# Reading the moving operand of split matmuls as four interleaved sets of 16-byte lines, with the weights at another address

## The chip, the cores and the metric

The kernel runs on one core of one Trainium2 chip. The metric is the device time of one execution in microseconds. Before the change it is 2151.36 us, the median of 3 runs (2151.3 to 2151.45).

## What is computed

Four batches of a channel attention are followed by a feed-forward layer. All data are float32.

```
B, N, C = 4, 6080, 256;  d_ff = 2048
qn = q / (norm of q over the rows + 1e-6);  kn likewise      # per batch and channel
s  = kn^T @ qn / tau                                         # 256 x 256 per batch
a  = softmax of s over its last axis
x  = v @ a                                                   # 6080 x 256 per batch
h  = x @ w_in                                                # 256 -> 2048
out = (h - tanh(h)) @ w_out                                  # 2048 -> 256
```

## The kernel before, in words

The kernel never forms x. For each batch it folds the attention matrix into the first weight (a @ w_in), so that the main loop multiplies v by a folded weight, applies h - tanh(h), and multiplies by w_out.

The work is cut into 192 slots: 4 batches, 6 pairs of column blocks of v, 8 slices of d_ff. A pair holds two blocks of 512 columns; the sixth pair of a batch holds two of 480. In one slot the first product is done as seven products of 128 x 128 weights with sums of v blocks (Strassen's scheme with Winograd's sums; `p1` to `p7` in `Quad.product`), which leave four results in the PSUM banks called x, y and z. ScalarE and VectorE add them up, apply tanh and the subtraction, and split the result g into two parts. The second product (`second`, L1173) multiplies the four results by w_out in 24 matmuls and gathers in the four banks ps_o.

Precision is kept by a split format: a float32 number is the sum of a high and a low part, both of type float32r (hi and lo tiles; gh and gl for g, f for the folded weight, wo_h and wo_l for w_out). A product of two split operands is three matmuls: high by low, high by high, low by high (`products`, L341 to L350). One slot thus issues 7 x 3 + 24 = 45 matmuls in the split format, each behind a weight load (LDWEIGHTS) of its own. A matmul streams its moving operand (128 partitions x 512 columns of 4 bytes) past the 128 x 128 weights that were loaded and writes 512 columns of one PSUM bank. Both the moving operand and the bank are walked in plain order of their columns before the change.

Other split matmuls are beside the slots: the scores s of later batches (ps_s, 256 columns wide, weights and moving operand both out of the tiles qh and ql), and the folding of later batches in groups (ps_w in `group_product`, 512 wide, weights in ef). Scores of batch 0 and some of batch 1 use plain float32 operands instead (the branch `wl is None` in `products`).

All weights and moving operands of the main loop lie, before the change, at multiples of 256 bytes in their partition; the unused tile `pad` (PAD = 208 floats) behind two small tiles sees to that. The folded weights come back from DRAM for each slot (`load_fold`, L835) into a ring of three buffers f.

The order of all instructions on all engines is written out by a planner (class `Plan`) at build time: it gives each instruction a price (`pe_cost` for matmuls, `act_cost`, `dve_cost`), a due time, and walks through the queue of each engine. The prices decide only the order. The order of the slots' products is fixed by the table ORDER; scores and other fills are put where the planner sees TensorE short of work.

Of the kernel before, what the change touches and what calls it, by code (L numbers as in the profile page):

```python
# [10 lines left out]
F32 = mybir.dt.float32  # L11
F32R = mybir.dt.float32r
# [6 lines left out]
P = 128  # L19
SQ = 32  # L20
GJ = 2
NMAX = 512
# [7 lines left out]
NS = 7  # L30
# [18 lines left out]
LEAD = 12  # L49
KEPT = 50.0  # L50
FIRST = 3
PAD = 208
LAG = 30
NORMS = 18

# [223 lines left out]


def pe_cost(n):
    return 0.0134 + n * 0.000417


@with_exitstack
def attn_moe(ctx: ExitStack, tc: tile.TileContext, qk, v4, qkT, tau, w_in, w_out, outT):
# [7 lines left out]
    B, N, _, C = qk.shape  # L294
    KC = C // P
    DFF = 2 * P * w_in.shape[0]
    NS2 = DFF // (2 * P)
# [5 lines left out]
    while s0 < N:  # L303
        n = min(NMAX, (N - s0) // 2)
# [7 lines left out]
    const = ctx.enter_context(tc.tile_pool(name="const", bufs=1))  # L312
# [4 lines left out]
    f_p = ctx.enter_context(tc.tile_pool(name="f_p", bufs=1))  # L317
    e_p = ctx.enter_context(tc.tile_pool(name="e_p", bufs=1))
# [3 lines left out]
    ring = {  # L322
        "wi": Ring(3), "f": Ring(3), "fa": Ring(1), "fb": Ring(1), "raw": Ring(3), "qh": Ring(2), "ql": Ring(2), "nt": Ring(2),
        "vraw": Ring(1), "vt": Ring(1), "vhl": Ring(8),
        "u": Ring(3), "c": Ring(4), "t": Ring(4), "gh": Ring(5), "gl": Ring(5), "ob": Ring(2),
    }

    def sb(pool, tag, shape, dtype, name):
        return pool.tile(list(shape), dtype, tag=tag, name=name, bufs=ring[tag].bufs)

    def bank(i, name, shape=(P, 512)):

        return ps_p.tile(list(shape), F32, tag=f"bank{i}", name=name)
# [3 lines left out]
    ones = const.tile([P, P], F32, name="ones")  # L337
    nc.vector.memset(ones, 1.0)

    def products(out, terms, first, last):  # L340

        seq = []
        for (wh, wl), (xh, xl) in terms:
            seq += [(wh, xh)] if wl is None else [(wh, xl), (wh, xh), (wl, xh)]
        for i, (w, x) in enumerate(seq):
            ins = nc.tensor.matmul(  # L346
                out, w, x,
                start=first and i == 0, stop=last and i == len(seq) - 1,
                skip_group_check=True,
            )  # L350
        return ins
# [3 lines left out]
    itau = const.tile([P, 1], F32, name="itau")  # L355
    const.tile([P, PAD], F32, name="pad")

# [7 lines left out]
        nc.vector.reciprocal(itau, ps_tau[0][:, 0:1])  # L365


    wo_h = const.tile([P, 2 * NS2, C], F32R, name="wo_h")
    wo_l = const.tile([P, 2 * NS2, C], F32R, name="wo_l")
    WN = 512  # L370

    class Convert:
# [74 lines left out]
    while j < NJ:  # L447
        n = min(GJ, NJ - j) if j >= SINGLES else 1
# [10 lines left out]
    class Attn:  # L459
# [218 lines left out]
                    nc.tensor.transpose(self.pt[:, kk, m * P:(m + 1) * P], self.e[:, m, kk * P:(kk + 1) * P], ident)  # L678

        def take_hi(self):  # L680
            self.ef = e_p.tile([P, 2, NS, P], F32R, name="ef")
            self.eh, self.el = (
                self.ef[:, j].rearrange("p n f -> p (n f)")[:, 0:KC * C].rearrange("p (k c) -> p k c", k=KC) for j in range(2)
            )
            nc.scalar.copy(self.eh, self.pt)
# [5 lines left out]
            nc.vector.tensor_scalar(self.e[:, m, :], self.e[:, m, :], self.rs[:, m:m + 1], None, op0=ALU.mult)  # L691

        def forms_hi(self):
            self.ef = e_p.tile([P, 2, NS, P], F32R, name="ef")
            nc.scalar.copy(self.ef[:, 0], self.fxe[:, 0:NS, :])

        def forms_lo(self):
# [69 lines left out]
        def fold_hi(self, s, part):  # L767
            gs = self.b * SLOTS + s
            if gs not in fold:
                fold[gs] = sb(f_p, "f", [P, 2, NS, P], F32R, f"f_{gs}")  # L770
            nc.scalar.copy(fold[gs][:, 0, part], self.fx[s][:, part, :])

        def fold_lo(self, s, part):
# [8 lines left out]
    fold = {}  # L782

    def where(gs):
        return gs // SLOTS, gs % SLOTS // NS2, gs % NS2
# [45 lines left out]

    def load_fold(gs):
        b, p, s = where(gs)
        fold[gs] = sb(f_p, "f", [P, 2, NS, P], F32R, f"f_{gs}")
        nc.sync.dma_start(fold[gs].bitcast(F32), fold_d[b, s])  # L835


# [45 lines left out]
    def plan_fold(b, s, z):  # L883
# [4 lines left out]
        for low, e in enumerate((a.ebuf, a.lbuf)):  # L888
            plan.add("PE", (8 - 4 * low) * pe_cost(FB), lambda low=low: a.fold(s, z, low), reads=[w, e], writes=[pw])
# [60 lines left out]
    def plan_group_product(b, group, k, z):  # L950
        a = ats[b]
        w = formbuf.pop((b, group, k))
        pw = Buf(z)
        which, _, takes = GROUP[k]
        name = f"{group}_{k}"
        plan.add("PE", 3 * pe_cost(NMAX), lambda: a.group_product(which, forms.pop((b, group, k)), z, name), reads=[w, a.ebuf, a.lbuf], writes=[pw])
        for to, plus in takes:
            fresh = (k, to) in ((0, (0, 0)), (1, (0, 1)))
            if fresh:
                a.fxbuf[to[1]] = Buf(ring[("fa", "fb")[to[1]]])  # L960
            plan.add(
                "DVE" if plus else "ACT", (dve_cost if plus else act_cost)(NMAX),
                lambda to=to, plus=plus, fresh=fresh: a.group_take(name, to, plus, fresh),
                reads=[pw] + ([a.fxbuf[plus[1]]] if plus and plus[1] != to[1] else []), writes=[a.fxbuf[to[1]]], port=False,
            )
# [176 lines left out]
    outs = {}  # L1142
    obufs = {}

    def second(quad, i):

        b, p, s, n = quad.b, quad.p, quad.s, quad.n
        row, c = i // 10 - 1, i % 10 - 1
        f = 2 * s + row
        gh, gl = quad.bufs["g", i]  # L1150
        key = b, p, c
        first = key not in obufs
        if first:
            obufs[key] = [0] + [Buf(3 + 2 * c + m) for m in range(KC)]
        done = obufs[key]
        done[0] += 1
        last = done[0] == 2 * NS2

        parts = (0, 1, 0, 0), (0, 0, 0, 1), (1, 1, 0, 0), (1, 0, 0, 1), (1, 0, 1, 2), (0, 0, 1, 2)
        end = last and b == B - 1 and p == NP - 1  # L1160
        if end:
            parts = parts[0:2] + parts[5:6] + parts[2:5]
        whole = slice(0, n)
        pieces = {m: [(whole, done[1 + m])] for m in range(KC)}
        if end and c:
            pieces[1] = [(slice(i * n // 2, (i + 1) * n // 2), Buf(f"end{i}")) for i in range(2)]
        todo = [(m, part, x, j, at_, to) for m, part, x, j in parts[0:3] for at_, to in pieces[m]] if end else []
        todo += [(m, part, x, j, at_, to) for at_, to in pieces[1] for m, part, x, j in parts[3:]] if end else [(m, part, x, j, whole, done[1 + m]) for m, part, x, j in parts]
        for m, part, x, j, at_, to in todo:
            def run(m=m, part=part, x=x, j=j, at_=at_):  # L1170
                if first and j == 0:
                    outs[key + (m,)] = bank(3 + 2 * c + m, f"ps_o_{b}_{p}_{c}_{m}")
                nc.tensor.matmul(  # L1173
                    outs[key + (m,)][:, at_], (wo_l if part else wo_h)[:, f, m * P:(m + 1) * P], quad.g[i][x][:, at_],
                    start=first and j == 0, stop=last and j == 2, skip_group_check=True,
                )

            plan.add("PE", pe_cost(at_.stop - at_.start), run, reads=[gl if x else gh, wobuf[s]], writes=[to])
            yield
        if last:  # L1180
            to_ = b * N + pairs[p][0] + c * n
            for m in range(KC):
                for k, (at_, src) in enumerate(pieces[m]):
                    ob = Buf(ring["raw" if c else "ob"])
                    tiles = {}

                    def copy(copy, m=m, k=k, at_=at_, tiles=tiles):
                        w = at_.stop - at_.start
                        if c:
                            raw = sb(qk_p, "raw", [P, GJ, 2, C], F32, f"ob_{b}_{p}_{c}_{m}_{k}")  # L1190
                            tiles[0] = raw[:, 0].rearrange("p x c -> p (x c)")[:, 0:w]
                        else:
                            tiles[0] = sb(g_p, "ob", [P, NMAX], F32, f"ob_{b}_{p}_{c}_{m}_{k}")[:, 0:w]
                        copy(tiles[0], outs[key + (m,)][:, at_])  # L1194

                    e = "ACT" if (m and len(pieces[m]) == k + 1) or not b and p < 2 else "DVE"
                    plan.add(
                        e, (act_cost if e == "ACT" else dve_cost)(at_.stop - at_.start),
                        lambda e=e, copy=copy: copy(nc.scalar.copy if e == "ACT" else nc.vector.tensor_copy),
                        reads=[src], writes=[ob],  # L1200
                    )
                    plan.add(
                        "SP", 0.35, lambda m=m, at_=at_, tiles=tiles: nc.sync.dma_start(outT[m * P:(m + 1) * P, to_ + at_.start:to_ + at_.stop], tiles[0]),
                        reads=[ob], size=0.26, due=plan.pe_time + 8.0,
                    )
# [248 lines left out]
    for gs in range(TOTAL):  # L1454
        quad = quads.pop(gs)
        for what in beside.get((gs, "start"), ()):
            what()
        for name, then in ORDER:
# [6 lines left out]
            for x in then:  # L1465
                if isinstance(x, int):
                    lag, x = max(0, lag - x), max(0, x - lag)
# [48 lines left out]
```

## Time and profile before

| what | value |
|---|---|
| median of 3 runs | 2151.36 us |
| span of the profiled execution, first to last instruction | 2150.2 us |
| time around the span (median less span) | 1.2 us |
| TensorE busy with matmuls | 2144.7 us, 100% of the span |
| VectorE busy | 1797.3 us, 84% |
| ScalarE busy | 1522.7 us, 71% |
| granted TensorE clock | 1.000 (2.4 GHz) |

[...] What one matmul costs is the distance between two starts. The chain of waits gives it at once: a piece of so many matmuls of one kind, divided by their number.

### The profile page before, as it was taken

What the parts mean: (1) busy time and instruction counts of PE and PEld (TensorE: products, weight loads), DVE (VectorE), ACT (ScalarE), POOL (GpSimd) and SP (SyncE); (2) the same over time, 40 slices, a digit from 0 to 9 for tenths busy, and PEclk for the clock granted to TensorE, in tenths of its full rate; (3) what the DMA queues carried; (4) which work ended last, traced back from release to release, by engine and by line L of the source; (5) the groups of instructions that cost most, each with busy time, mean ns of one, the idle gap of its engine ahead of it and who ended that gap; (6) DMA issues with size and microseconds to landing.
All of it is one profiled execution on the core that took longest, in us unless ns stands there. A gap on an engine that the chain in (4) does not pass through costs nothing.

```text
span 2150.2 us, 28567 instructions
## 1 busy us (share of the span) xinstructions
PE 2144.7 (100%) x9859; PEld 1803.2 (84%) x9859; DVE 1797.3 (84%) x2959; ACT 1522.7 (71%) x2729; POOL 3.3 (0%) x11
## 2 busy tenths in 40 slices
PE   9999999999999999999999999999999999999999
PEld 8888888888888888888888888888888888888888
DVE  7998888899888787788988778878889878778776
ACT  5667788767677777766767778766676666666665
POOL 0000000000000000000000000000000000000000
PEclk9999999999999999999999999999999999999999
DMA  9855576455564555425656445443464432332331
GB/s 386 301 194 185 170 284 241 145 192 194 186 251 173 188 179 188 176 98 182 220 174 247 165 184 208 155 165 112 169 240 160 157 125 89 139 125 86 134 113 53
DMA packets 99907, 383.55 MB, mean 178 GB/s; under 512 B 11442, under 2 KB 20146, under 8 KB 97202
## 3 DMA queue, kind: packets, MB, share of 16 engines
q1 hardware_dynamic: 99762, 381.73, 49.5%
q8 instruction: 78, 1.28, 0.2%
q14 instruction: 67, 0.55, 0.1%
HBM read 315.88 MB, written 65.80 MB: 178 GB/s over the span
## 4 chain that ended last, share of the span: by engine, by line
PE 99%; DMA 0%; SPq 0%; DVE 0%; ACT 0%; issue 0%
PE ps_o L1173 48%; PE x L346 24%; PE y L346 12%; PE ps_s L346 7%; PE z L346 6%; PE ps_w L346 1%; PE ps_w L744 1%; DMA vhl<-qk_dram 0%; SPq L526 0%; PE ps_n L518 0%; PE ps_b L628 0%; PE ps_t L678 0%; DVE ob L1194 0%; ACT ob L1194 0%; PE ps_tau L362 0%
## 5 line engine op out<-in xcount | busy, mean ns | idle before, releaser
L346 PE MATMUL x<-v,f 128*128 128x512 f32 (+1 forms) x2304 | 613.7, 388 | 0.0
L1173 PE MATMUL ps_o<-gh,wo_h 128*128 128x512 f32 (+1 forms) x1537 | 595.6, 388 | 0.0
L1173 PE MATMUL ps_o<-gh,wo_l 128*128 128x512 f32 (+1 forms) x1537 | 595.2, 387 | 0.0
L1107 DVE TENSOR_TENSOR gl<-t,gh 128x512 fp32r<-128x512 f32 (+1 forms) x768 | 516.5, 680 | 90.6 <-ACT gh L1103 87.6
L1103 ACT CAST gh<-t 128x512 fp32r<-128x512 f32 (+1 forms) x768 | 468.9, 618 | 145.4 <-DVE t L1099 136.7
L346 PEld LDWEIGHTS x<-v,f 128*128 128x128 f32 x2304 | 432.3, 188 | 87.2 <-ACT fa L753 0.4
L1095 ACT ACTIVATE t<-c 128x512 f32<-128x512 f32 (+1 forms) x576 | 361.7, 628 | 190.1 <-DVE c L1083 184.9
L1173 PE MATMUL ps_o<-gl,wo_h 128*128 128x512 f32 (+1 forms) x1537 | 471.5, 388 | 0.0
L1099 DVE TENSOR_TENSOR t<-c,t 128x512 f32<-128x512 f32 (+1 forms) x576 | 392.1, 682 | 92.0 <-ACT t L1095 82.8
L1173 PEld LDWEIGHTS ps_o<-gh,wo_l 128*128 128x128 f32 x1537 | 288.6, 188 | 56.9
L1173 PEld LDWEIGHTS ps_o<-gl,wo_h 128*128 128x128 f32 x1537 | 288.6, 188 | 56.5
L1173 PEld LDWEIGHTS ps_o<-gh,wo_h 128*128 128x128 f32 x1537 | 288.7, 188 | 55.6
L346 PE MATMUL y<-v,f 128*128 128x512 f32 (+1 forms) x1152 | 321.6, 387 | 0.0
L1067 ACT COPY u<-x 128x512 f32<-128x512 f32 (+1 forms) x384 | 223.5, 582 | 130.1 <-PE x L346 128.5
L1083 DVE TENSOR_TENSOR c<-u,y 128x512 f32<-128x512 f32 (+1 forms) x384 | 259.5, 676 | 20.6 <-ACT u L1067 10.8
L346 PEld LDWEIGHTS y<-v,f 128*128 128x128 f32 x1152 | 216.2, 188 | 43.1
L1095 ACT ACTIVATE t<-x 128x512 f32<-128x512 f32 (+1 forms) x192 | 113.9, 593 | 97.8 <-PE x L346 97.3
L1099 DVE TENSOR_TENSOR t<-x,t 128x512 f32<-128x512 f32 (+1 forms) x192 | 131.3, 684 | 60.1 <-ACT t L1095 58.8
L1083 DVE TENSOR_TENSOR c<-p,z 128x512 f32<-128x512 f32 (+1 forms) x192 | 130.5, 680 | 51.7 <-PE z L346 47.8
L346 PE MATMUL z<-v,f 128*128 128x512 f32 (+1 forms) x576 | 160.9, 387 | 0.0
L346 PEld LDWEIGHTS z<-v,f 128*128 128x128 f32 x576 | 108.1, 188 | 21.6
L1067 ACT COPY p<-x 128x512 f32<-128x512 f32 (+1 forms) x192 | 112.0, 584 | 2.3 <-PE x L346 0.9
(139 smaller groups left out, 1444.6 us busy)
## 6 DMA issues: line engine op xcount, KB each, us to landing
f<-f_d SPq DMA_DIRECT2D x184, 896.0 KB, 4.6
nt<-qkT_dram SPq DMA_DIRECT2D x96, 380.0 KB, 5.4
raw<-qk_dram SPq DMA_DIRECT2D x47, 512.0 KB, 5.8
wf<-wf_d SPq DMA_DIRECT2D x42, 512.0 KB, 4.0
f_d<-fe SPq DMA_DIRECT2D x48, 448.0 KB, 3.5
vraw<-v_dram SPq DMA_DIRECT2D x20, 1024.0 KB, 7.6
outT_dram<-ob SPq DMA_DIRECT2D x80, 256.0 KB, 3.0
vhl<-qk_dram SPq DMA_DIRECT2D x14, 512.0 KB, 9.2
```

The source lines that it names most:

```text
L346: ins = nc.tensor.matmul(out, w, x, start=first and i == 0, stop=last and i == len(seq) - 1, skip_group_check=True,)
L744: nc.tensor.matmul(self.pw[s][:, m, :], e[:, kk, m * P:(m + 1) * P], w[:, x, kk, :], start=not (low or m or kk or x), stop=bool(low and m ...
L1067: nc.scalar.copy(self.tiles[to], self.tiles["X"][:, 0:self.n])
L1083: nc.vector.tensor_add(self.tiles[i], self.tiles[u], self.tiles[ps][:, 0:self.n])
L1095: nc.scalar.activation(self.tiles["t", i], self.tiles[c][:, 0:n], AF.Tanh)
L1099: nc.vector.tensor_sub(x, self.tiles[c][:, 0:n], x)
L1103: nc.scalar.copy(self.g[i][0], self.tiles["t", i])
L1107: nc.vector.tensor_sub(self.g[i][1], self.tiles["t", i], self.g[i][0].bitcast(F32))
L1173: nc.tensor.matmul(outs[key + (m,)][:, at_], (wo_l if part else wo_h)[:, f, m * P:(m + 1) * P], quad.g[i][x][:, at_], start=first and j == ...
```

## The change

A helper `in_sets` turns 512 columns into four sets. Set 0 holds columns 0 to 3, 16 to 19, 32 to 35 and so on, set 1 columns 4 to 7, 20 to 23 and so on: four columns of 4 bytes are a line of 16 bytes, and a set takes every fourth line. A split matmul then streams set 0, 1, 2 and 3 one after another, and writes the columns of the bank in that same order, so that each result lies where it lay before. The number of matmuls, their widths and their operands are the same. Only split matmuls are changed; those with plain float32 operands, and the folding of batch 0 at L744, keep the plain order.

The tiles of the weights (f, ef, wo) are made a little longer and their contents begin 4 floats in; with PAD, `pad_wo` and `pad_f` all weights of the slots and of the group products then lie 48 bytes past a multiple of 256, while the moving operands stay at multiples of 256. The weights of the scores (qh, ql) stay at multiples of 256 too. wo_h and wo_l become two halves of one tile.

The planner's price of a 512-wide matmul falls by 0.0067 us, which changes the order that it writes.

```
-PAD = 208
+PAD = 24
+SHIFT = 4
...
 def pe_cost(n):
-    return 0.0134 + n * 0.000417
+    return (0.0067 if n == NMAX else 0.0134) + n * 0.000417
...
+    def in_sets(x):
+        return x.rearrange("p (a b c) -> p b a c", b=4, c=4)
...
             ins = nc.tensor.matmul(
-                out, w, x,
+                *((out, w, x) if wl is None else (in_sets(out), w, in_sets(x))),
...
-    wo_h = const.tile([P, 2 * NS2, C], F32R, name="wo_h")
-    wo_l = const.tile([P, 2 * NS2, C], F32R, name="wo_l")
+    def shifted(pool, extra, shape, **named):
+        pitch = 1
+        for x in shape:
+            pitch *= x
+        t = pool.tile([P, pitch + extra], F32R, **named)
+        return t[:, SHIFT:SHIFT + pitch].rearrange("p (a n f) -> p a n f", a=shape[0], n=shape[1])
+
+    wo = shifted(const, 16, (2, 2 * NS2, C), name="wo")
+    wo_h, wo_l = wo[:, 0], wo[:, 1]
+    const.tile([P, 40], F32, name="pad_wo")
+    f_p.tile([P, 8], F32, name="pad_f")
...
-            self.ef = e_p.tile([P, 2, NS, P], F32R, name="ef")
+            self.ef = shifted(e_p, 8, (2, NS, P), name="ef")
...
-        fold[gs] = sb(f_p, "f", [P, 2, NS, P], F32R, f"f_{gs}")
+        fold[gs] = shifted(f_p, 64, (2, NS, P), tag="f", name=f"f_{gs}", bufs=ring["f"].bufs)
...
                 nc.tensor.matmul(
-                    outs[key + (m,)][:, at_], (wo_l if part else wo_h)[:, f, m * P:(m + 1) * P], quad.g[i][x][:, at_],
+                    in_sets(outs[key + (m,)][:, at_]), (wo_l if part else wo_h)[:, f, m * P:(m + 1) * P], in_sets(quad.g[i][x][:, at_]),
```

On TensorE the order of the matmuls changes in one place, in slots 1 and 2 of batch 0. In the rows, x, y, z and ps_o are banks, v, gh and gl moving operands, ps_s the scores of batch 1 (a step is four records of plain float32). Before:

```order
L346 MATMUL x_0_0_1_703<-v5_0_0_563,f_1_635 128x512 x3
L346 MATMUL ps_s_1_393<-qh_1_15_642 128x256 x4
L346 MATMUL x_0_0_2_836<-v0_0_0_478,f_2_675 128x512 x3
L1173 MATMUL ps_o_0_0_1_1_811<-gh22_0_0_0_727,wo_h_95 128x512
L346 MATMUL y_0_0_1_753<-v6_0_0_487,f_1_635 128x512 x3
```

and now:

```order
L350 MATMUL x_0_0_1_704<-v5_0_0_564,f_1_636 128x4x32x4 x3
L350 MATMUL x_0_0_2_820<-v0_0_0_479,f_2_676 128x4x32x4 x3
L1186 MATMUL ps_o_0_0_1_1_810<-gh22_0_0_0_728,wo_95 128x4x32x4
L350 MATMUL y_0_0_1_754<-v6_0_0_488,f_1_636 128x4x32x4 x3
L1186 MATMUL ps_o_0_0_1_1_810<-gl22_0_0_0_741,wo_95 128x4x32x4
```

The score step with qh_1_15 moved from before the first product of slot 2 to before that of slot 3. On ScalarE, VectorE and the DMA queue the same instructions stand in an order that differs by a place or two here and there. VectorE in slot 1, before (c is a sum of banks, t the tanh and then g, gl the low part of g, a_wo the conversion of w_out):

```order
L1099 TENSOR_TENSOR t11_0_0_1_768<-c11_0_0_1_758,t11_0_0_1_768 128x512
L1083 TENSOR_TENSOR c22_0_0_1_796<-u3_0_0_1_775,y_0_0_1_753 128x512
L394 TENSOR_SCALAR a_wo1_788<-a_wo1_788 128x512
L395 SCALAR_TENSOR_TENSOR a_wo1_788<-raw_wo1_470,a_wo1_788 128x512
L1107 TENSOR_TENSOR gl11_0_0_1_813<-t11_0_0_1_768,gh11_0_0_1_799 128x512
```

and now:

```order
L1096 TENSOR_TENSOR c22_0_0_1_788<-u3_0_0_1_770,y_0_0_1_754 128x512
L1112 TENSOR_TENSOR t11_0_0_1_785<-c11_0_0_1_762,t11_0_0_1_785 128x512
L407 TENSOR_SCALAR a_wo1_790<-a_wo1_790 128x512
L408 SCALAR_TENSOR_TENSOR a_wo1_790<-raw_wo1_471,a_wo1_790 128x512
L1120 TENSOR_TENSOR gl11_0_0_1_816<-t11_0_0_1_785,gh11_0_0_1_807 128x512
```

The sum c22 moved ahead of the subtraction t11.

## Rows read from the trace of the kernel before

**Rows 1.** The page's head: span, busy time of TensorE (PE) and VectorE (DVE)

```profile
span 2150.2 us, 28567 instructions
PE 2144.7 (100%) x9859; PEld 1803.2 (84%) x9859; DVE 1797.3 (84%) x2959; ACT 1522.7 (71%) x2729; POOL 3.3 (0%) x11
```

**Rows 2.** Waits of PE: who for whom, total us, times, longest

```profile
PE warm L1383 <- DVE ones L338: 1.1, 1, 1.1
PE ps_s L346 <- DMA vhl<-qk_dram: 0.5, 1, 0.5
```

**Rows 3.** The page's chain that ended last, share of the span by engine

```profile
PE 99%; DMA 0%; SPq 0%; DVE 0%; ACT 0%; issue 0%
```

**Rows 4.** The chain in order of time: start us, length us, what, matmuls

```profile
72.51 3.45 PE ps_s L346 x16
...
157.52 2.04 PE ps_o L1173 x9
...
749.30 1.43 PE ps_s L346 x12
750.74 0.93 PE ps_o L1173 x4
...
2134.59 1.95 PE ps_o L1173 x9
```

**Rows 5.** PE's groups by shape: line, operands, shapes, count, busy us, mean ns

```profile
L346 PE MATMUL x<-v,f 128*128 128x512 f32 x1920 | 515.4, 390 | 0.0
L1173 PE MATMUL ps_o<-gh,wo_h 128*128 128x512 f32 x1280 | 498.6, 390 | 0.0
...
L346 PE MATMUL y<-v,f 128*128 128x512 f32 x960 | 269.6, 389 | 0.0
L346 PE MATMUL z<-v,f 128*128 128x512 f32 x480 | 134.8, 389 | 0.0
L346 PE MATMUL x<-v,f 128*128 128x480 f32 x384 | 99.4, 378 | 0.0
L1173 PE MATMUL ps_o<-gh,wo_h 128*128 128x480 f32 x255 | 96.5, 378 | 0.0
...
L346 PE MATMUL ps_s<-qh,ql 128*128 128x256 f32 x198 | 56.0, 283 | 0.0
...
L346 PE MATMUL y<-v,f 128*128 128x480 f32 x192 | 51.9, 378 | 0.0
L346 PE MATMUL ps_w<-wf,ef 128*128 128x512 f32 x126 | 35.6, 391 | 0.0
...
L346 PE MATMUL z<-v,f 128*128 128x480 f32 x96 | 26.0, 379 | 0.0
```

**Rows 6.** Weight loads (PEld) by shape: count, busy us, mean ns

```profile
L346 PEld LDWEIGHTS x<-v,f 128*128 128x128 f32 x2304 | 432.3, 188 | 87.2 <-ACT fa L753 0.4
...
L346 PEld LDWEIGHTS ps_s<-vhl 128*128 128x128 f32 x120 | 23.1, 195 | 4.8 <-DMA vhl<-qk_dram 1.6
```

**Rows 7.** Busy time by stretch: us, then each engine's busy us (instructions), clock, DMA

```profile
50.00:200.00 150.00, 150.00 (x729) 128.08 (x728) 145.69 (x277) 105.24 (x195) 0.52 (x1) 1.00 0.65 234
120.00:130.00 10.00, 10.00 (x47) 8.57 (x46) 9.86 (x21) 5.57 (x10) 0.00 (x0) 1.00 0.39 127
350.00:400.00 50.00, 50.00 (x223) 41.39 (x222) 48.30 (x86) 39.67 (x77) 0.00 (x0) 1.00 0.69 249
```

**Rows 8.** The page's DMA issues: count, KB each, median us to landing

```profile
f<-f_d SPq DMA_DIRECT2D x184, 896.0 KB, 4.6
```

More of the change, by code (lines that the diff above doesn't have):

```diff
@@ L693, in forms_hi @@
         def forms_hi(self):
-            self.ef = e_p.tile([P, 2, NS, P], F32R, name="ef")
+            self.ef = shifted(e_p, 8, (2, NS, P), name="ef")
             nc.scalar.copy(self.ef[:, 0], self.fxe[:, 0:NS, :])
@@ L833, in load_fold @@
         b, p, s = where(gs)
-        fold[gs] = sb(f_p, "f", [P, 2, NS, P], F32R, f"f_{gs}")
+        fold[gs] = shifted(f_p, 64, (2, NS, P), tag="f", name=f"f_{gs}", bufs=ring["f"].bufs)
         nc.sync.dma_start(fold[gs].bitcast(F32), fold_d[b, s])
```

## The prediction

> **What bounds the kernel now.** I read the page's head first: PE is busy for 2144.7 us of a span of 2150.2 us [rows 1]. Such a share can hide waits, because a matmul's record lasts longer than its turn; so the waits of PE come next. There are two, 1.6 us in all, both in the first microseconds [rows 2], and the chain that ended last is 99% PE [rows 3]. PE is never short of work. The time is the sum of the distances between starts of matmuls, and a change to that distance is worth its full size until another engine takes over. VectorE with 1797.3 us is the nearest, 347 us below PE over the whole run [rows 1], though not in every stretch [rows 7].
>
> Next I ask what one matmul costs and how much of it is columns. The granted clock is 1.00, the 2.4 GHz level [rows 7], so a column takes 0.4167 ns. The chain in order of time gives the distances [rows 4]:
> - 512 wide, split: 2.04 us for 9 is 226.7 ns. The columns take 213.3, so 13.3 ns are excess, 32 cycles.
> - 480 wide, split: 1.95 us for 9 is 216.7 ns. Columns 200.0, excess 16.7.
> - 256 wide, split: 1.43 us for 12 is 119.2 ns. Columns 106.7, excess 12.5.
> - 256 wide, plain float32: 3.45 us for 16 is 215.6 ns. That is two cycles per column, 213.3, and an excess of 2.3.
>
> Two things stand out. The excess of the split matmuls does not grow with the width, so it belongs to the matmul or to its weight load, not to the columns. And it is not one fixed price: right behind the 256-wide run four 512-wide matmuls take 0.93 us, 232.5 ns each [rows 4], and the 480-wide ones pay more than the 512-wide. The plain matmuls, which take an element in only every second cycle, pay almost nothing for the same 512 bytes of weights. This looks like a collision: the next weights are read while the moving operand streams at one element per cycle, and what the two readers lose depends on where each of them is. 128 weights of 4 bytes are 32 lines of 16 bytes, and 32 cycles are lost. I infer it; no row shows a memory.
>
> [...]
>
> **The change part by part.** *Streaming in four sets, weights 48 bytes off.* It touches these matmuls [rows 5]: 512 wide, 1920 of x, 960 of y, 480 of z, 126 of ps_w and three groups of 1280 of ps_o (one is shown): 7326. 480 wide: 384 of x, 192 of y, 96 of z and three groups of 255 of ps_o: 1437. 256 wide: three groups of 198 of ps_s, 594.
>
> What can be won lies between nothing and the excess. All of it down to the plain matmuls' 2.3 ns would be 11.0 ns x 7326 = 80.6 us, 14.4 x 1437 = 20.7 us and 10.2 x 594 = 6.1 us: 107 us. The other end is below nothing, since no row shows a matmul that streams or writes anything but plain columns; its price is under the third rival. If the excess is collisions, a set helps like this: while one set streams (128 columns, 53 ns), only every fourth line of the weights can be in its way. A load is recorded with 188 ns [rows 6], 3.5 sets long, so it meets several sets, but each of them with a quarter of its lines. If each line met its own set once only, 8 of the 32 cycles would stay, a gain of 10 ns. But the 480-wide and the post-score rows show that phases wander and cost up to 19 ns. No row decides between nothing and 10 to 13 ns. I take the middle of the excess, 6.7 ns: 7326 x 6.67 = 48.9 us. The 480-wide sets are 120 columns long and their phases wander already; I give them half of that, 3.3 x 1437 = 4.8 us, with bounds of 0 and 20.7. The scores' weights stay where they were; I give them nothing (0 to 6.1).
>
> *Weight loads.* 188 ns per load [rows 6] stays under the new 220 ns distance, so loads don't take over. The start at 48 bytes leaves 32 lines of 16 bytes. I cost it at nothing.
>
> *Writing the folded weights off the 256 mark.* The DMA of f now lands at 48 bytes past. It takes 4.6 us [rows 8]; a slot is 45 x 226.7 ns = 10.2 us, and f is asked for two slots ahead in a ring of three. Even twice as long it would be covered.
>
> *The planner's order.* PE's list differs in one score step that goes a slot later; the step depends on nothing that is late, and PE is not idle there: nothing. VectorE's, ScalarE's and the DMA queue's lists differ by neighbours that changed places, such as the sum c22 ahead of t11. What hides these is the slack of VectorE and ScalarE, so I look where there is none: in 50 to 200 us VectorE is busy for 145.7 of 150 us, and in 120 to 130 us for 9.86 of 10 [rows 7]. That stretch has 729 matmul records, so PE would gain at most 729 x 6.67 ns = 4.9 us there, and VectorE has 4.3 us to give, but not in each slot. I let 3 us of the gain be lost there as waits of PE for VectorE, and 1 us in stretches like 350 to 400 us, where VectorE is at 48.3 of 50 and PE's 50 fall to 50 - 223 x 6.67 ns = 48.5. Elsewhere (VectorE at 84% on the mean) 2 or 3% less PE time leaves room.
>
> *Sum.* Against the span of the profiled execution: 2150.2 - 48.9 - 4.8 + 4 = 2100.5 us. The median of the runs is 1.2 us above the span, so the forecast is 2101.7, say **2102 us**. Its own range, from 5 to 8.5 ns per 512-wide matmul with 480-wide between 0 and 8 ns, is 2082 to 2119.
>
> **Rivals.**
> *1. Nearly all of the excess goes.* For it: plain matmuls show that the weights can be loaded for 2.3 ns. Against: they take an element every second cycle, which leaves gaps that a split matmul hasn't. Price: 107 us less; in the 150 us stretch PE would need up to 729 x 11.0 ns = 8 us less, 142, below VectorE's 145.7, so I put the waits at 8 us there and elsewhere. 2151.4 - 107 + 8 = 2052 us. Chance 0.12.
>
> *2. The excess is a fixed price of changing weights.* Then sets change nothing, and the time stays at 2151, at most 2 us above from an order that was planned for a faster PE. For it: 32 cycles recur at 512 and, nearly, at 256 columns. Against: the 232.5 and the 216.7 ns rows, and the plain matmuls, which change weights as often. Chance 0.10.
>
> *3. Jumping costs more than colliding: slower.* Before, a matmul reads and writes one run of 2048 bytes; now it makes 128 jumps on both sides, one behind every fourth column. If each costs one cycle, 0.417 ns, a 512-wide matmul pays 53.3 ns, a 480-wide 50.0, a 256-wide 26.7: 391 + 72 + 16 = 479 us, 2630 us. It decides from a small size on: with the forecast's 6.7 ns won, the kernel is slower as soon as a matmul loses 7.3 ns to its jumps, 18 cycles over 128 jumps. The far end is a matmul at two cycles per column, as the plain ones run [rows 4]: 7326 x 213 ns is 1.56 ms more. For it: no row has a broken pattern on PE, so nothing excludes it. Against: within a jump's length the 16 bytes are still read in one piece, and PE at one element per cycle crosses from line to line just as often as before. Chance 0.18.
>
> [...]
>
> **How the numbers follow.** Forecast 0.60, nearly all 0.12, fixed price 0.10, jumps 0.18. A measurement of this kernel tells from no change what is over 0.2%, 4.3 us. Faster is the forecast and the first rival, 0.72; same is the second, 0.10; slower the third, 0.18. The range holds 8 in 10 with the forecast, the fixed price and most of the first rival: 2055 to 2153 us. What it leaves out is nearly all the third.
>
> **What would show it.** Right: pieces of nine ps_o at 1.98 us in place of 2.04, nine 480-wide ones at about 1.92, the 256-wide at 119 ns as before, still no waits of PE beyond a few us, and those between 50 and 200 us on VectorE. Wrong: nine ps_o at 2.04 (fixed price), at 1.94 (nearly all gone), or above 2.04 (jumps); or the shorter distance with PE's share well below 99% and waits for VectorE all over, by which the sum's 4 us would be the step that failed.

## The result and the profile after

The changed kernel takes 2114.66 us, the median of 4 runs (2113.9 to 2116.3), against 2151.38 before: a ratio of 0.983, with a 95% interval of 0.9816 to 0.9844. It is 36.7 us faster. The forecast was 2102 us, 49.7 us faster. The time lies inside the stated range and in the upper part of the forecast's own, which reached to 2119.

The head and the chain's shares of the changed kernel's page (they answer to [rows 1] and [rows 3]):

```profile
span 2112.1 us, 28460 instructions
PE 2103.7 (100%) x9859; PEld 1804.1 (85%) x9859; DVE 1795.8 (85%) x2959; ACT 1523.8 (72%) x2729; POOL 3.3 (0%) x11
...
PE 93%; DVE 5%; ACT 1%; DMA 1%; issue 0%; SPq 0%; ACTq 0%
```

The span fell by 38.1 us and PE's busy time by 41.0; VectorE (DVE) works as long as before. PE is still what the time is made of, but 7% of the chain now runs through other engines. The chain in order of time gives the distances, as in [rows 4] (start us, length us, what, matmuls):

```profile
92.77 1.87 PE ps_o L1186 x8
...
749.34 1.40 PE ps_s L350 x12
750.73 0.91 PE ps_o L1186 x4
...
755.61 1.98 PE ps_o L1186 x9
...
2096.40 1.98 PE ps_o L1186 x9
```

Nine 512-wide matmuls take 1.98 us in place of 2.04: 220.0 ns each, 6.7 ns less. Nine 480-wide ones (the last row) also take 1.98, where they took 1.95: 220.0 ns, 3.3 ns more. The twelve of the scores fell from 1.43 to 1.40. The four behind them need 0.91 us, 228 ns each: the 512-wide distance is not yet back at 220. And the first row shows a stretch that holds another distance: behind twelve matmuls of the folding of batch 0, 45 512-wide matmuls in a row, from 88.9 to 99.4 us, stand 233.3 ns apart.

The waits of PE, all of them (us in total, times, longest us), and the busy stretch (they answer to [rows 2] and [rows 7]):

```profile
PE ps_w L350 <- ACT fx L744: 1.1, 3, 0.4
PE warm L1396 <- DVE ones L339: 1.1, 1, 1.1
PE x L350 <- PE x L350: 0.9, 3, 0.3
PE ps_s L350 <- DMA vhl<-qk_dram: 0.7, 1, 0.7
PE x L350 <- ACT gh L1116: 0.6, 1, 0.6
PE ps_o L1186 <- DVE gl L1120: 0.3, 1, 0.3
```

```profile
50.00:200.00 150.00, 149.13 (x732) 128.26 (x731) 146.49 (x278) 106.04 (x195) 0.52 (x1) 1.00 0.65 235
```

Four new lines, 2.9 us: at the start of the group products of each later batch (ps_w, three times), some 26 us behind it (x, three times), and between 175 and 180 us, where VectorE is full (busy for 11.93 of 12 us from 169 to 181).

Adding up the distances between starts over the whole trace gives a balance that closes. The 7326 matmuls of 512 columns take 1664.5 us before and 1625.3 after, 39.2 less; the 1437 of 480 columns 311.5 and 314.2, 2.7 more; the 594 split ones of 256 columns 2.1 less; everything else 0.6 more. Together that is 38.0 us less.

### The profile page after: what moved, and what is told of

Same layout as the page of the kernel before. It is cut to its first block, busy times and chain, and to the rows that moved or that the text cites. A ratio compares the mean times of both kernels' runs of the same rounds, so it can differ in the third digit from the quotient of the medians.

```text
span 2112.1 us, 28460 instructions
## 1 busy us (share of the span) xinstructions
PE 2103.7 (100%) x9859; PEld 1804.1 (85%) x9859; DVE 1795.8 (85%) x2959; ACT 1523.8 (72%) x2729; POOL 3.3 (0%) x11
## 4 chain that ended last, share of the span: by engine, by line
PE 93%; DVE 5%; ACT 1%; DMA 1%; issue 0%; SPq 0%; ACTq 0%
PE ps_o L1186 45%; PE x L350 23%; PE y L350 11%; PE ps_s L350 7%; PE z L350 6%; DVE t L1112 1%; PE ps_w L350 1%; DVE gl L1120 1%; DVE c L1096 1%; DMA raw_wi<-w_in_dram 0%; DVE ex L660 0%; PE ps_w L757 0%; ACT gh L1116 0%; DMA vhl<-qk_dram 0%; DVE ef L711 0%
## 5 line engine op out<-in xcount | busy, mean ns | idle before, releaser
L1186 PE MATMUL ps_o<-gh,wo 128*128 128x512 f32 (+1 forms) x3074 | 845.1, 381 | 0.0
L1186 PEld LDWEIGHTS ps_o<-gh,wo 128*128 128x128 f32 x3074 | 576.6, 188 | 96.7
L350 PE MATMUL x<-v,f 128*128 128x512 f32 (+1 forms) x2304 | 602.2, 381 | 1.5 <-PE x L350 0.9
L1186 PE MATMUL ps_o<-gl,wo 128*128 128x512 f32 (+1 forms) x1537 | 463.1, 381 | 0.3 <-DVE gl L1120 0.3
L1186 PEld LDWEIGHTS ps_o<-gl,wo 128*128 128x128 f32 x1537 | 289.2, 188 | 50.0 <-DVE gl L1120 1.0
L350 PE MATMUL y<-v,f 128*128 128x512 f32 (+1 forms) x1152 | 315.5, 381 | 0.0
L350 PEld LDWEIGHTS y<-v,f 128*128 128x128 f32 x1152 | 216.5, 188 | 37.4 <-DVE c L1096 0.3
L598 ACT ACTIVATE nt<-nt 128x760 f32<-128x760 f32 x96 | 80.1, 834 | 0.0
L350 PE MATMUL ps_s<-qh 128*128 128x256 f32 x290 | 76.6, 309 | 0.0
```

Source lines behind the costliest of these rows:

```text
L350: ins = nc.tensor.matmul(*((out, w, x) if wl is None else (in_sets(out), w, in_sets(x))), start=first and i == 0, stop=last and i == len(s ...
L598: nc.scalar.activation(x, x, AF.Square, accum_out=self.squares[:, row, part:part + 1])
L1186: nc.tensor.matmul(in_sets(outs[key + (m,)][:, at_]), (wo_l if part else wo_h)[:, f, m * P:(m + 1) * P], in_sets(quad.g[i][x][:, at_]), st ...
```

## The experiments

Each variant of the kernel was timed against the kernel before on the same chip; streams are single runs of kernels that hold nothing but matmuls.

### One half of the change alone: sets without the shift

The kernel before, with `in_sets` and the new price of the change:

```
 PAD = 208
...
+    def in_sets(x):
+        return x.rearrange("p (a b c) -> p b a c", b=4, c=4)
...
```

> The order of reading and writing of the change, and its planner's price, with the weights left at multiples of 256. Theory, collision: only part of the gain, 2115 to 2151 us, 512-wide distances between 220 and 226.7 ns. Rival, order alone: 2115 us, 220 ns. Rival, address alone: 2151 us, 226.7 ns.

Measured: 2138.46 us, 0.9939 of before (0.9924 to 0.9953). The distances do not settle. In the chain, nine matmuls of ps_o take 2.00 to 2.04 us, beside longer pieces, and over all 512-wide matmuls the distances without waits have a mean of 225.8 ns, most of them between 220 and 239. The 480-wide ones do well (last row):

```profile
179.21 2.21 PE ps_o L1176 x9
...
210.97 2.00 PE ps_o L1176 x9
...
323.30 2.04 PE ps_o L1176 x9
...
2121.46 1.89 PE ps_o L1176 x9
```

So the order alone is worth 13 us, a good third. Little of it comes from the 512-wide matmuls: their distances add up to 5.0 us less than before, the 480-wide to 5.2 and the scores' to 3 us. 1.89 us for nine is 210.0 ns: with the weights at 0, four sets are the best that was seen for 480 columns.

### The other half alone: the shift without the sets

The changed kernel with plain order:

```
     def in_sets(x):
-        return x.rearrange("p (a b c) -> p b a c", b=4, c=4)
+        return x
```

> The weights 48 bytes past multiples of 256 and the planner's price of the change, with plain order of reading and writing. Theory, collision: both are needed, so 2150 to 2155 us and 226.7 ns per 512-wide matmul. Rival, address alone: 2115 us and 220 ns.

Measured: 2196.54 us, 1.0209 of before (1.0194 to 1.0224), 45 us slower. No theory had that. Nine 512-wide matmuls take 2.10 us, 233.3 ns each, and nine 480-wide 1.94, 215.6 ns:

```profile
169.82 2.10 PE ps_o L1186 x9
...
2179.83 1.94 PE ps_o L1186 x9
```

Over the whole trace the 512-wide distances add up to 46.0 us more than before and the 480-wide to 1.5 less, which is the loss. The address matters by itself, and at 48 bytes it is bad for plain order (233.3 ns against 226.7 at 512 columns) and good for sets (220.0 ns, where the sets alone had a mean of 225.8). The two halves give -13 and +45 us alone and -37 together: the change is one thing, not a sum of two.

### The distance by itself: streams of one kind

Streams of 64 matmuls, one kind behind the other, with the weights at 16 addresses; the letter is the address past a multiple of 256 bytes in steps of 16 (a is 0, d is 48):

> This kernel leaves out the whole computation: it is nothing but streams of 64 split-format matmuls of one kind, one stream behind another, each matmul with a weight load of its own; what is read is the distance between starts in each stream. Streams differ in the order of reading and writing (plain; four sets of 16-byte lines; sets on the reading side alone; sets on the writing side alone; four sets of 8-byte lines; two sets; eight sets), in the width (512, 480, 256), and in where the weights start past a multiple of 256 bytes (0, 16, ... 240). Theory, collision: the distance depends on the order of reading and on the address of the weights, and not on the order of writing; plain 226.7 ns and four sets with weights 48 bytes past 220.0 ns at 512 columns, sets on the reading side alone 220, on the writing side alone 226.7. Rival, address alone: plain with weights at 48 already 220. Rival, order alone: four sets 220 at every address. Rival, PSUM: sets on the writing side alone slower than plain, four sets of 8-byte lines slower than of 16-byte lines; by the jump price of the prediction up to 53 ns.

The chain of that kernel (wide is 512 columns, mid 480; read and write have sets on one side alone; eight has lines of 8 bytes, two and many are two and eight sets; 64 matmuls a row, so 14.08 us are 220.0 ns and each 0.43 us 6.7 ns more):

```profile
52.79 14.09 PE wide_sets_d L91 x64
66.88 14.52 PE wide_sets_e L91 x64
...
240.94 14.54 PE wide_plain_a L91 x64
...
284.91 14.93 PE wide_plain_d L91 x64
...
492.32 14.53 PE wide_write_a L91 x64
506.85 29.53 PE wide_eight_a L91 x64
536.38 14.93 PE wide_two_a L91 x64
551.32 15.78 PE wide_many_a L91 x64
567.10 14.09 PE wide_read_d L91 x64
581.19 14.93 PE wide_write_d L91 x64
...
684.53 13.47 PE mid_sets_a L91 x64
...
725.57 13.86 PE mid_sets_d L91 x64
```

Of the 16 addresses only 48 gave the sets 220 ns; the others gave 223 to 232. Plain order was at 226.7 at 0, 16 and 240 and at 229 to 234 elsewhere. The kernel before and the change each sit at an address that was best for their order here; each stream was run once, behind one other stream, and further down that turns out to matter. Sets on the reading side alone do all of it (read_d as sets_d), sets on the writing side alone do nothing (write_a as plain_a, write_d as plain_d). Four sets are better than two or eight: eight sets of the same 16-byte lines took 246.5 ns, 20 more than plain order. 8-byte lines double the time, 461 ns.

Address alone and order alone are out, and so is the PSUM rival for runs of 16 bytes. What 8-byte lines cost was then asked of each side:

> Again nothing but streams of 64 matmuls of one kind, the whole computation left out. The weights start 48 bytes past a multiple of 256 (letter d) or at it (a), the moving operand at 0, 16, ... 240 bytes past it (from_a to from_p), at widths 512 and 480; then the 480-wide sets at every address of the weights, 8-byte lines on the reading side alone and on the writing side alone, and sets of longer lines. Theory, collision between weight reads and moving reads: what counts is where the two stand to each other, so the 480-wide stream that was at 210 ns with both operands at 0 comes back near 210 for some start of the moving operand while the weights stay at 48; 512 columns are best at 0 with 220. Eight-byte lines: if the doubling to 461 ns is SBUF's, it is on the reading side alone (461) and the writing side alone stays at 226.7; by a PSUM rule it is the other way round. Rival, address of the weights alone: the start of the moving operand changes nothing, 220 and 216.7 to 220 throughout.

```profile
242.25 13.66 PE mid_from_a L83 x64
...
283.51 13.66 PE mid_from_d L83 x64
...
502.40 13.87 PE mid_sets_d L83 x64
...
695.84 29.53 PE wide_eightread_a L83 x64
725.37 14.54 PE wide_eightwrite_a L83 x64
...
784.85 17.67 PE wide_most_a L83 x64
```

The price of 8-byte lines is all on the reading side (29.53 us for 64, 461 ns each); writing in runs of two columns is free (14.54 us against 14.52 in plain order), as writing in runs of 16 bytes was in the streams above (14.53 against 14.54). Sixteen sets of 16-byte lines (wide_most) took 276 ns, so not every order of 16-byte runs is cheap. Moving operand and weights both at 48 gave 213.3 ns at 480 columns (mid_from_d). But mid_from_a and mid_sets_d are the same stream, and took 213.3 and 216.7. The 210 ns that the theory expected to see again for some start of the moving operand did not come: the 16 starts gave 212 to 220. At 512 columns the start counts: starts at 0 and 144 bytes gave 220.0 ns, the others 223 to 243.

### Does it go by the line of weights?

With 64 and 32 columns of weights in place of 128, and with other types:

> Streams of 64 matmuls once more, 512 columns wide, the whole computation left out, with fewer weights per matmul: 128 columns of weights (512 bytes a partition, full), 64 (half), 32 (quarter), in plain order and in four sets, weights at 0 (a) and 48 bytes (d) past a multiple of 256; then the same with bfloat16 and with plain float32 operands. Theory, collision: what is lost over the columns' 213.3 ns is paid per line of weights that is read, so plain order at 0 loses 13.3 ns with 128 weights, 6.7 with 64 and 3.3 with 32 (226.7, 220.0, 216.7 ns); bfloat16 moves half the bytes per column and loses 3 ns or less in any order; plain float32 stays at 2 x 213.3 + 2.3 per pass or so in any order. Rival, a fixed price per change of weights: 226.7 ns at 128, 64 and 32 weights, and 13 ns with bfloat16 too.

The chain (half and quarter are 64 and 32 columns of weights; the view cuts long names on the left):

```profile
24.56 14.32 PE split_full_sets_a L81 x64
38.88 14.72 PE split_half_plain_a L81 x64
53.60 13.87 PE split_half_sets_a L81 x64
67.47 14.81 PE plit_quarter_plain_a L81 x64
...
110.38 13.81 PE alf_precision_sets_a L81 x64
124.19 54.93 PE float_plain_a L81 x128
...
249.00 14.94 PE split_full_sets_d L81 x64
```

The theory falls in its simple form. In plain order a quarter of the weights does not cost a quarter: 230 and 231 ns for half and quarter, even more than 226.7 for all. In sets with the weights at 0 half of them did shorten the distance, from 223.8 to 216.8 ns, the least of any 512-wide split stream, but a quarter took 223.0 again; with the weights at 48 it was 233.4, 220.0 and 222.0, which tells less, since all 128 columns held 220.0 there in other runs. But it is no fixed price of changing weights either: bfloat16 takes 215.8 ns and plain float32 429.1 per record (two cycles a column, 426.7), both 2.5 ns over their columns, with as many changes and in either order. Of the three types only float32r, whose streams take 4 bytes in nearly every cycle (512 columns in 544 cycles at 226.7 ns), has the larger excess, 3.5 to 20.1 ns here. And the last row is a surprise: the 512-wide sets with weights at 48, 220 ns in two runs, are at 233.4 here.

### The same stream behind different ones

> Streams of 64 matmuls, the whole computation left out. Four kinds are read (512 wide in four sets with weights at 48; 512 wide plain with weights at 0; 480 wide in four sets with weights at 48 and the moving operand at 0; the same with the moving operand at 48), each of them behind four different streams (x: 512 plain, weights at 48; y: 512 in sets, weights at 32; z: 480 in sets, weights at 0; s: 256 in sets, weights at 0). Theory, settling: one and the same stream keeps the distance into which the stream ahead of it brought it, so the 512-wide sets come out at 233.3 ns behind x, as in the run before, and at 220.0 behind y, as in the first run of streams, and the 480-wide ones at one of 213.3, 216.7 and 220.0. Rival, the distance belongs to the stream and its addresses: one value for each kind, whatever is ahead (220.0 or 233.3, 226.7, 216.7, 213.3).

```profile
24.34 14.92 PE widesets_x L75 x64
...
53.77 14.12 PE widesets_y L75 x64
67.88 13.47 PE ahead_widesets_z L75 x64
81.35 14.11 PE widesets_z L75 x64
...
102.91 14.12 PE widesets_s L75 x64
...
131.95 14.52 PE wideplain_x L75 x64
...
160.99 14.54 PE wideplain_y L75 x64
175.53 13.66 PE ahead_wideplain_z L75 x64
```

Behind x the 512-wide sets stay at 233.3 ns for all 64 matmuls, behind y, z and s they fall to 220.0 within a few. So this stream has two distances that hold, 33 and 35 times 16 cycles, and what was ahead decides which. The plain one came out at 226.7 and the 480-wide ones with the weights at 48 at 216.5 to 216.8 (moving operand at 0) and 213.3 (at 48) behind all four. The stream ahead called z shows the same with 480 columns: three times it took 210.4 ns on the mean, behind sets, and 213.4 behind plain 512-wide matmuls (ahead_wideplain_z). The 45 matmuls at 233.3 ns in the changed kernel show the same two distances inside the kernel.

### Waits: the planner's old price

```
-    return (0.0067 if n == NMAX else 0.0134) + n * 0.000417
+    return 0.0134 + n * 0.000417
```

> The change with the planner's old price of a 512-wide matmul, so that the order of instructions is that of before while the matmuls run at the new distance. If the waits of PE that the change shows at the start of the group products and around 175 us come from the new order, they go, and the time falls by up to 5 us to 2110. If they come from VectorE and ScalarE being late for a faster PE, they stay or grow: 2114 to 2122 us.

Measured: 2110.52 us (0.981 of before, 0.9794 to 0.9827), 4.1 us below the change. TensorE's matmuls now stand in the order of before, one by one. PE's waits by the profile are down to 2.4 us from 4.7:

```profile
PE warm L1396 <- DVE ones L339: 1.1, 1, 1.1
PE x L350 <- ACT fa L766: 0.7, 1, 0.7
PE ps_w L350 <- ACT fx L744: 0.4, 1, 0.4
PE ps_s L350 <- DMA vhl<-qk_dram: 0.2, 1, 0.2
```

Most of the new waits came from the new order, not from a VectorE too slow for the faster PE.

### 480 columns: plain, or moved

Both on top of the old price. In the first, `in_sets` returns x unchanged unless it is 512 or 256 columns wide. In the second the moving operands of 480 columns start 12 floats in:

```
-            self.hi[i], self.lo[i] = (x[:, j, 0:self.n] for j in range(2))
+            at_ = 0 if self.n == NMAX else 12
+            self.hi[i], self.lo[i] = (x[:, j, at_:at_ + self.n] for j in range(2))
```

(and gh and gl likewise)

> The change with the planner's old price, and with the 480-wide matmuls back in plain order of reading and writing. Theory, collision: four sets are a loss at 480 columns with weights at 48 and the moving operand at 0, 218.6 ns on the mean in the changed kernel against 215.8 ns in the run with plain order and weights at 48; 1437 matmuls x 2.8 ns = 4 us below the run with the old price, 2106 to 2107 us. Rival, sets are no loss there and the 218.6 ns come from waits and order: no change, 2110 to 2111 us.

> The change with the planner's old price, and with the moving operands of the 480-wide matmuls starting 48 bytes past a multiple of 256, as their weights do; the sets stay. Theory, what counts is where the two readers stand to each other: the stream of this kind took 213.3 ns, so 1437 x 5.3 ns = 7.6 us less than the old price alone, 2103 us. Rival, the address of the weights alone decides: 218.6 ns as before, 2110 to 2111 us. Third possibility: the stream can settle at several distances, as this one did between 213.3, 216.7 and 220.0 ns with the moving operand at 0, and settles elsewhere in the kernel: 2104 to 2112 us.

> The run before this one with the planner's price of a 512-wide matmul halfway between the old one and that of the change (0.0100 us beside the columns). If the waits come from the distance between price and chip in either direction, a price in the middle leaves least of them and the time is 0 to 2 us below the run before, 2101 to 2103 us. Rival, the waits are a matter of how the order happens to fall: 2100 to 2108 us, with waits at other places.

Measured: plain 2103.57 us (0.9777 of before, 0.9762 to 0.9791), moved 2099.72 (0.9759, 0.9744 to 0.9773), moved with the price in the middle 2100.02 (0.9759, 0.9743 to 0.9776). The 480-wide pieces of nine, in the plain and in the moved kernel:

```profile
2085.95 1.94 PE ps_o L1188 x9
```

```profile
2082.49 1.92 PE ps_o L1188 x9
```

The mean distance of the 480-wide matmuls is 218.6 ns in the change, 215.5 in plain order and 212.9 moved; 1437 times the difference is 4.5 and 8.2 us. The measured 6.9 and 10.8 us, against the run with the old price, are more, and both times lie below what was expected, because the 512-wide distances without waits also fell, from 220.9 to 220.5 ns, 2.8 us over 7326. With the old price alone, 512-wide matmuls between 480-wide ones hold 236 to 237 ns in each batch, twelve and nine in a row; with the 480-wide ones plain or moved those stretches are gone. The middle price gave nothing. The moved kernel beats the kernel before by 52.0 us, as timed beside it, and the change by 15.

## Why the prediction was right, and where it was not

**What bounds the kernel: right.** PE set the time before and sets it after; 38.1 us of span fell out of the distances between matmuls, and their balance closes within 0.1 us.

**6.7 ns per 512-wide matmul: right in size, with a reason that was half wrong.** The distance fell from 226.7 to 220.0 ns, exactly the middle of the excess that was taken. But the middle was a choice between ends, not a result, so that it fits to a tenth of a nanosecond is luck. The working behind it, weight lines that collide with the moving stream one by one, does not stand: fewer lines did not cost less in proportion, in plain order not less at all, and the same stream held 220 or 233. What stands is that the larger excess was seen in float32r streams alone (bfloat16 and plain float32 had 2.5 ns), went by the order of reading and not of writing (with the weights at 48, sets on the reading side alone took 220 ns and on the writing side alone 233.3, as plain order), and depended on the addresses (226.7 to 233.3 ns in plain order with the weights at 0 and 48) and on what ran ahead (220.0 or 233.3). [Rows 7] give the clock as 1.00 and no frequency; that a column takes 0.4167 ns is shown by the streams, where plain float32 less bfloat16, 429.1 less 215.8 ns, is 213.3 ns for 512 columns.

**48.9 us from it: too much by 9.6, of which 4.4 were not in the sum.** The steady distance gives 7326 x 6.67 = 48.9 us. The mean without waits is 221.0 ns, not 220.0, while before it was 227.1 against 226.7: after a run of scores the distance needs some matmuls to come back, between 480-wide matmuls it holds 236 ns for up to twelve, and behind the folding of batch 0 it held 233.3 for 45. That costs 0.6 ns on the mean, 4.4 us. The trace of before had the row (232.5 ns behind the scores), and the prediction used it only for the mechanism. The other 5.2 us of the 512-wide ones are distances over 250 ns, PE's waits with the slow restart behind each (at 460 us the distances run 728, 333, 222 ns); the sum had 4 for that.

**480-wide, 4.8 us won: the step that failed.** They lost 2.7 us, outside the bounds of 0 and 20.7 that the prediction gave the term. It took half of the 512-wide gain because the distances at 480 vary already, and had no room for a loss from the new address. The streams showed why the gain doesn't carry over: at 480 columns the sets take 210.0 ns with the weights at 0 (213.3 behind plain order) and 213.3 with both operands at 48, and with weights at 48 and the operand at 0, which is what the change has, they lay at 213.3 and 216.7 in the streams and in the kernel mostly at 220.0. Moving the operand gave it back. The term was 7.5 us off, most of the 11.6 us by which the span missed the sum; the 512-wide ones with their waits make 5.7, the rest 0.6, and the 256-wide take 2.1 off.

**256-wide, nothing: off by 2.1 us.** The sets alone shorten these, with the weights where they were: in streams with the weights at 0 from 120 to 113.5 ns.

**The order: 4 us of waits, measured 5.2.** The sum comes out near by luck: what is over 220 ns in these distances is 1.7 us at 175 to 180 us with VectorE full, where the prediction looked and put 3, and 3.7 at the group products of later batches, which it did not name. The old price showed that the order makes most of them.

**Weight loads and the writing of f, at nothing: right.** The busy time of the loads is 1804.1 us against 1803.2, and f lands in 4.6 us as before.

**The rivals.** Nearly all gone: no stream of 512-wide split matmuls with all 128 columns of weights was below 220. Fixed price: out, by the change itself, by bfloat16 and by plain float32 (2.5 ns over their columns), and by the address of the weights, which alone moved plain order from 226.7 to 233.3 ns. Jumps that cost: out for the four sets of 16 bytes of the change, on both sides, but not for every order of such runs, since eight and sixteen sets took 246.5 and 276 ns. Runs of 8 bytes cost on the reading side, where a column takes 0.90 ns, close to the far end of two cycles that the rival named.

## What to carry to other kernels

Read what a matmul costs from the distance between starts in the chain, and take the columns off; in this kernel and its variants the rest was 7 to 24 ns in float32r (220.0 to 237 ns at 512 columns) and could be moved by the order of reading and by where operands start, together. Measure such a layout as a stream of its own at each width that the kernel has, and behind what stands ahead of it in the kernel, because the best address for one order or width was among the bad ones for another (48 bytes at 512 columns: 220.0 ns in sets, 233.3 in plain order). When a faster engine comes with a new order of work, time the old order too.

## What was not expected of the hardware

- Many split streams settle at a mean distance on a grid of 3.33 ns, 8 cycles: 210.0, 213.3, 216.7, 220.0, 226.7, 233.3 ns. Some do so matmul by matmul, some as the mean of a pattern that repeats (213 to 224 ns around 216.7); others lie between (222.5, 225.5 ns).
- The same stream held 220.0 or 233.3 ns for 64 matmuls, depending on what ran ahead of it, and the changed kernel has 45 in a row at 233.3 ns amid 220.0. Why is open: no run shows how the reads of the weights and of the moving operand meet, and the collision remains an inference.
- Writing PSUM in four sets of runs of 8 or 16 bytes was free (14.54 and 14.53 us for 64 matmuls, against 14.52 and 14.54 in plain order); reading the moving operand in runs of 8 bytes doubled the time (461 ns for 512 columns).
- Loads of 64 and 32 columns of weights did not shorten the distance of float32r streams in plain order (230 and 231 ns against 226.7 for 128); in sets with the weights at 0, 64 columns did (223.8 to 216.8 ns), 32 hardly (223.0).
